# Splitting two tile drains and reordering one: tiles 3 and 7 in halves, V pair 4 ahead of a gelu

## Chip, cores, metric

One core of a Trainium2 chip. The metric is the device time of the whole program in microseconds (us), median of several executions. "Span" is the time from the first to the last instruction in a profile; it is some 1.7 us shorter than the metric.

## The reference

`x` is 2048 tokens by 448 features, bf16. It is normalised, and the result goes through a linear attention (A) and a shifted MLP (B):

```python
xn = layernorm(x)
# A: 16 heads of 28
q, k, v = split(xn @ wqkv)
phi(t)  = concat(softmax(t @ w_phi), softmax(-t @ w_phi))
o       = (phi(q) @ (phi(k).T @ v)) / (phi(q) @ phi(k).sum() + 1e-6)
# B
h  = gelu(layernorm(xn) @ w1)           # quarters of h shifted by 1, -1, 2, -2 tokens
x1 = xn + shift(h) @ w2
out = x + o @ wo + x1 + gelu(layernorm(x1) @ w3) @ w4
```

The change lies in the opening stretch, about 7 to 17 us: xn is transposed tile by tile, and `xn @ wv` ("V pairs" of two 128-token tiles) and `xn @ w1` ("WA", "WC", "WD": blocks of w1's columns, for groups of four tiles) run as the tiles arrive.

## The kernel before

The kernel records all instructions for five engines in program order and derives the semaphores from the buffers that they touch. Nothing is timed: each engine works through its own list, and what one line of the list costs depends on what it waits for.

Transposes of one tile go through TensorE into a pair of PSUM banks (eight small ones, in two row halves), and ScalarE copies them to `xnT`:

```python
def xn_t(i, b, j=0):                       # b: bank pair
    t = pairs[b][:, :].bitcast(BF16).rearrange("p (h x) -> p h x", h=2)
    for kc in range(KC):                   # KC = 4
        at = 256 * j + 64 * kc
        for h, (lo, hi) in enumerate((LO, HI)):
            R.tr(t[:, h, at:at + 64], xn[lo:hi, i, 128 * kc:128 * kc + 128], ident[lo:hi, lo:hi])

def xn_e(i, b, n=1, eng="ACT", cuts=(0, KC)):
    ...
                for c0, c1 in zip(cuts, cuts[1:]):
                    R.act(to[:, c0:c1], fr[:, c0:c1], ACT.Copy)
```

A V pair accumulates two tiles in the two banks of its pair. Matmuls of the lower and the upper 64 rows run side by side, in different banks; then they swap banks ("late"):

```python
def early():
    row_pairs(side(0, LO, (0, 1)), side(1, HI, (0, 1)), True)
    if i > 3:
        mid()
def mid():
    row_pairs(side(0, LO, (2, 3)), side(1, HI, (2, 3)))
return early, lambda: row_pairs(side(1, LO, (0, 1, 3)), side(0, HI, (0, 2, 3))), mid
```

`V(i, 0)`, `V(i, 2)`, `V(i, 1)` are early, middle and late. `v_out` is ScalarE's drain of a V pair, `wa_out` and `wc_out` are gelus that drain w1's blocks. The bank pairs: tile 7's transposes and V pair 6 both use pair 3; V pair 4 and tiles 8, 9 use pair 2; WA of groups 0 and 1 use pair 0.

The dependency tracker keeps PSUM by bank: a write to a bank waits for every reader and writer of that bank on another engine, and a matmul on one row half waits for the other half's last write to the same bank.

```python
vps = {i: v_pair(i, b) for i, b in ((0, 2), (2, 3), (4, 2), (6, 3), (8, 2), (10, 2), (14, 3))}
play([(spin, 3, 256), (xn_T, 2, 0), V(0, 0), (xn_T, 3, 1), V(0, 2), V(0, 1),
      V(2, 0), V(2, 2), (v_out, 0, 2), (xn_T, 4, 1), WA(0, 0),
      V(2, 1), (v_out, 2, 3), (xn_T, 5, 2), WA(0, 1), WC(0, 0), (xn_T, 6, 3), WC(0, 1), (wc_out, 0, 1),
      V(4, 0), (xn_T, 7, 3), (wa_out, 0, 0), V(4, 1), (v_out, 4, 2), V(6, 0),
      WC(1, 0), V(6, 1), (v_out, 6, 3), (xn_T, 8, 2, 2), WA(1, 0), ...])
```

The softmax here doesn't subtract the row's maximum and nothing guards it: scores larger than these inputs give would overflow.

## Time and profile before

| | before |
|---|---|
| device time, median of 3 | 173.45 us (173.34 to 173.59) |
| span in the profile | 171.7 us |
| TensorE busy | 167.9 us, 98% |
| ScalarE busy | 83.7 us, 49% |

TensorE bounds the kernel. How to read such a profile here: a matmul's record is longer than what it occupies of the array, so gaps of TensorE are counted from start to start. A bracket at the end of a row of the timeline gives the idle time of that engine before the row and what ended it. Weight loads ("PEld") run ahead of matmuls, so their idle time is an upper bound of what the array lost.

The prediction below shows TensorE's rows. ScalarE's, from the timeline of the kernel before (start, length, engine, line, operation, output from input, shapes), are what parts two and three of the change rearrange:

```profile
14.38 0.60 ACT L208 ACTIVATE xnT<-bank 128x512 bf16<-128x512 bf16 x1 [0.16 <-PE bank L204]
14.87 1.02 ACT L208 ACTIVATE hT<-bank 128x1024 bf16<-128x1024 f32 x1
15.78 0.92 ACT L208 ACTIVATE vaug<-bank 128x896 bf16<-128x896 f32 x1
17.01 0.92 ACT L208 ACTIVATE vaug<-bank 128x896 bf16<-128x896 f32 x1 [0.31 <-PE bank L200]
```

The rows are tile 7's copy, the gelu of w1 group 0, the drain of V pair 4 and that of V pair 6. The gelu stands between tile 7's copy and V pair 4's drain.

### The profile page before, as it was taken

The page shows a single profiled execution, that of the slowest core. Times are in us where ns is not written, and L with a number is a line of the kernel's source. Part 1 is how long each engine was busy: PE and PEld are TensorE (multiplying, and loading weights), DVE is VectorE, ACT ScalarE, POOL GpSimd, SP SyncE. Part 2 cuts the span into 40 slices and gives each one's busy share as a digit, 9 for nine tenths or more (in the row PEclk, how much of TensorE's full clock was granted, in tenths as well). Part 3 has the DMA queues.
Part 4 walks back from the last instruction along what each step waited for, and adds up shares of the span by engine and source line. Part 5 has one row for each costly group of instructions (what it writes and reads, how often), then busy time and mean ns, then how long its engine had stood idle before and what let it go on. Part 6 is the DMA issues. An engine that isn't in the chain of part 4 may idle for free.

```text
span 171.7 us, 5220 instructions
## 1 busy us (share of the span) xinstructions
PE 167.9 (98%) x2269; PEld 89.9 (52%) x2269; DVE 112.6 (66%) x259; ACT 83.7 (49%) x102; POOL 91.6 (53%) x130
## 2 busy tenths in 40 slices
PE   7999999999999999999999999999999999999994
PEld 5455576444555554554545555545545555545553
DVE  4799986368999999837678953446417425474621
ACT  4868863988777887847225222224203222224000
POOL 3676560024799999750749388540721714523740
PEclk9999999999999999999999999999999999999999
DMA  4996541239943011122103732035311220314331
GB/s 131 320 270 86 135 102 42 55 45 376 379 144 64 4 31 34 31 46 50 34 2 75 79 63 60 30 86 107 80 36 50 61 57 4 84 31 34 84 88 53
DMA packets 32679, 15.21 MB, mean 89 GB/s; under 512 B 23952, under 2 KB 32016, under 8 KB 32656
## 3 DMA queue, kind: packets, MB, share of 16 engines
q1 hardware_dynamic: 32224, 14.62, 34.9%
q8 instruction: 18, 0.29, 0.8%
q10 hardware_dynamic: 432, 0.26, 0.5%
q14 instruction: 5, 0.04, 0.1%
HBM read 7.14 MB, written 1.84 MB: 52 GB/s over the span
## 4 chain that ended last, share of the span: by engine, by line
PE 94%; DVE 2%; issue 1%; POOL 1%
PE bank L200 93%; PE bank L204 1%; POOL rs L212 1%; DVE vaug L212 1%; DVE st L212 0%; DVE xn L212 0%; POOL mv L212 0%; DVE mv L212 0%; DVE gT L212 0%
## 5 line engine op out<-in xcount | busy, mean ns | idle before, releaser
L208 ACT ACTIVATE phik<-bank 128x1024 bf16<-128x1024 f32 (+1 forms) x44 | 42.3, 984 | 60.3 <-PE bank L200 60.2
L200 PE MATMUL bank<-gT,w 64*128 64x512 bf16 x392 | 50.0, 377 | 0.0
L212 DVE TENSOR_TENSOR vaug<-bank,vaug 128x464 f32<-128x464 f32 (+3 forms) x65 | 32.7, 512 | 22.5 <-PE bank L200 20.9
L200 PE MATMUL bank<-w,phik 64*128 64x448 bf16 (+3 forms) x434 | 45.2, 343 | 0.0
L212 POOL TENSOR_TENSOR xnT<-vaug 128x196 bf16<-128x196 f32 (+1 forms) x32 | 18.1, 587 | 45.4 <-DVE vaug L212 45.4
L200 PEld LDWEIGHTS bank<-w,phik 64*128 64x128 bf16 (+1 forms) x434 | 22.4, 94 | 20.8 <-issue 0.4
L645 POOL TENSOR_TENSOR phik<-phik,rks 128x1792 bf16<-128x1792 bf16 (+1 forms) x9 | 25.8, 2877 | 11.1 <-DVE rks L212 10.3
L200 PEld LDWEIGHTS bank<-gT,w 64*128 64x128 bf16 x392 | 17.6, 94 | 17.5 <-ACT phik L208 0.4
L212 POOL TENSOR_TENSOR vaug<-xn,xtok 128x448 f32<-128x448 bf16 x16 | 16.2, 1034 | 0.2 <-DVE vaug L212 0.2
L212 DVE TENSOR_REDUCE ksum<-phik 128x64 f32<-128x1792 bf16 x8 | 16.1, 2011 | 0.0
L212 DVE RECIPROCAL vaug<-bank 128x16 f32<-128x16 f32 x16 | 4.1, 257 | 17.8 <-PE bank L200 17.8
L212 POOL TENSOR_TENSOR rs<-mv,mhalf 128x1 f32<-128x1 f32 (+2 forms) x20 | 13.1, 658 | 3.3 <-DVE mv L212 1.8
L200 PE MATMUL bank<-xnT,wpq 64*128 64x512 bf16 x112 | 14.7, 376 | 0.0
L200 PE MATMUL bank<-wo,xnT 64*128 64x448 bf16 (+3 forms) x110 | 13.6, 343 | 0.0
L200 PE MATMUL bank<-wv,xnT 64*128 64x448 bf16 x112 | 13.2, 350 | 0.1
L200 PE MATMUL bank<-w,hT 64*128 64x448 bf16 x112 | 13.2, 349 | 0.0
L200 PE MATMUL bank<-wpk,xnT 64*128 64x448 bf16 x112 | 13.2, 349 | 0.0
L200 PE MATMUL bank<-xnT,w 64*128 64x512 bf16 (+2 forms) x168 | 12.6, 306 | 0.0
L212 DVE TENSOR_TENSOR xn<-bank,xn 128x512 bf16<-128x512 f32 (+1 forms) x16 | 9.2, 619 | 3.0 <-PE bank L200 3.0
L208 ACT ACTIVATE hT<-bank 128x512 bf16<-128x512 f32 (+1 forms) x10 | 7.4, 770 | 4.0 <-PE bank L200 4.0
L212 DVE BATCH_NORM_STATS2 st<-xn 128x6 f32<-128x448 bf16 x16 | 9.3, 580 | 0.0
L212 POOL TENSOR_SCALAR g_tok<-xn,rs 128x512 bf16<-128x512 bf16 x12 | 9.1, 772 | 0.3
(68 smaller groups left out, 166.7 us busy)
## 6 DMA issues: line engine op xcount, KB each, us to landing
w<-in_B_w_dram SPq DMA_DIRECT2D x2, 896.0 KB, 5.8
out_dram<-vaug SPq DMA_DIRECT2D x15, 112.0 KB, 1.9
w<-in_B_w_dram SPq DMA_DIRECT2D x1, 1568.0 KB, 11.2
xtok<-in_A_x_dram SPq DMA_DIRECT2D x2, 448.0 KB, 6.0
wv<-in_A_wqkv_dram SPq DMA_DIRECT2D x2, 224.0 KB, 4.4
xtok<-in_A_x_dram SPq DMA_DIRECT2D x2, 224.0 KB, 4.7
w<-in_B_w_dram SPq DMA_DIRECT2D x2, 224.0 KB, 4.8
wo<-in_A_wo_dram SPq DMA_DIRECT2D x2, 224.0 KB, 6.7
```

The costliest lines, as they stand in the source:

```text
L200: self.op("PE", lambda e: e.matmul(out, lhsT, rhs, start=start, stop=stop, skip_group_check=True), [out], [lhsT, rhs], tile=self._tile(lhsT))
L204: self.op("PE", lambda e: e.transpose(out, in_, ident), [out], [in_, ident], tile=self._tile(in_))
L208: self.op("ACT", lambda e: e.activation(out, in_, func, **kw), [out], [in_] + aps)
L212: self.op(eng, lambda e: getattr(e, name)(out, *args, **kw), [out], aps)
L645: R.op(pool, lambda e, h=h: e.tensor_tensor(ph[:, h, :], ph[:, h, :], rb[:, h, :], op=ALU.mult), [ph[:, h, :]], [ph[:, h, :], rk, *(g_tok[ ...
```

## The change

The intent: give TensorE tile 3's first half sooner and use the second half to fill a wait; let V pair 6 start on tile 7's first half; free V pair 4's banks before the gelu, since tile 8 needs them.

```diff
-        def xn_t(i, b, j=0):
+        def xn_t(i, b, j=0, cut=(0, KC)):
...
-            for kc in range(KC):
+            for kc in range(*cut):
...
+        def xn_Th(i, b, *cut):
+            xn_t(i, b, 0, cut)
+            xn_e(i, b, cuts=cut)
...
-        play([(spin, 3, 256), (xn_T, 2, 0), V(0, 0), (xn_T, 3, 1), V(0, 2), V(0, 1),
+        play([(spin, 3, 256), (xn_T, 2, 0), V(0, 0), (xn_Th, 3, 1, 0, 2), V(0, 2), (xn_Th, 3, 0, 2, KC), V(0, 1),
...
-              V(4, 0), (xn_T, 7, 3), (wa_out, 0, 0), V(4, 1), (v_out, 4, 2), V(6, 0),
+              V(4, 0), (lambda: xn_T(7, 3, cuts=(0, 2, KC)),), V(4, 1), (v_out, 4, 2),
+              (wa_out, 0, 0), V(6, 0),
```

## The prediction

> **What bounds the kernel now.** I read the engine table of the page first, then the chain of work that ended last, then the waits inside the stretch that the change touches, then the timeline of that stretch engine by engine. The engine table and the clock row of the page:
>
> ```profile
> PE 167.9 (98%) x2269; PEld 89.9 (52%) x2269; DVE 112.6 (66%) x259; ACT 83.7 (49%) x102; POOL 91.6 (53%) x130
> PEclk9999999999999999999999999999999999999999
> ```
>
> TensorE is busy for 98% of the span. The clock row must be read beside it: no slice is throttled, so nothing is to be had from the clock. The chain in order of time (start, length, what):
>
> ```profile
> 6.87 0.42 DVE xn L212
> 7.29 0.05 issue
> 7.33 0.29 PE bank L204 x8
> ...
> 19.32 4.28 PE bank L200 x60
> 23.60 0.23 PE bank L204 x16
> 23.84 145.65 PE bank L200 x1943
> ```
>
> From 7.33 us on the chain stays on TensorE to 169.49 us. All edits lie between about 7.8 and 17 us. The change adds and removes no matmul and no transpose, so all that it can win is idle time of TensorE inside that stretch, and only if a later wait doesn't take it back. The waits between 7 and 24 us (total, times, longest):
>
> ```profile
> PEld bank L204 <- DVE xn L212: 1.0, 3, 0.4
> PEld bank L200 <- PE bank L200: 0.5, 1, 0.5
> PEld bank L200 <- ACT xnT L208: 0.4, 1, 0.4
> PEld bank L204 <- issue: 0.3, 1, 0.3
> PEld bank L204 <- DVE wpk L212: 0.2, 1, 0.2
> ```
>
> These are waits of the weight loads, which run ahead of the matmuls; the array loses less. I count the loss from matmul starts: a pair of 448-column matmuls on the two row halves occupies 0.19 us (V pair 4's second step starts pairs at 14.29, 14.48 and 14.67), though each is recorded as 0.35 long. The places, from the timeline:
>
> ```profile
> 7.85 0.17 PEld L204 LDWEIGHTS bank<-ident,xn 64*128 64x128 bf16 x8 [0.29 <-DVE xn L212]
> 8.58 1.06 PEld L200 LDWEIGHTS bank<-wv,xnT 64*128 64x128 bf16 x14 [0.50 <-PE bank L200]
> 9.51 0.41 DVE L212 TENSOR_SCALAR xn<-xtok,mv,rs 128x512 bf16<-128x512 bf16 x1 [0.23 <-POOL rs L212]
> 9.97 0.17 PEld L204 LDWEIGHTS bank<-ident,xn 64*128 64x128 bf16 x8 [0.33 <-DVE xn L212]
> 15.03 0.11 PEld L200 LDWEIGHTS bank<-wv,xnT 64*128 64x128 bf16 x4 [0.44 <-ACT xnT L208]
> 16.81 0.32 PEld L204 LDWEIGHTS bank<-ident,xn 64*128 64x128 bf16 x16 [0.29 <-issue]
> 23.41 0.31 PEld L204 LDWEIGHTS bank<-ident,xn 64*128 64x128 bf16 x16 [0.24 <-DVE wpk L212]
> ```
>
> Real array gaps: 0.22 us before 8.58 (last pair of V pair 0's middle step starts at 8.17, so the array is free at 8.36); 0.05 before 9.97 (9.73 + 0.19); 0.17 before 15.03 (14.67 + 0.19); 0.04 before tile 8's first transpose at 16.84 (16.61 + 0.19); 0.06 before 23.41 (23.16 + 0.19). Together 0.54 us, 0.3% of 173.45. That bounds the gain before anything else is asked: 2% would be 3.5 us.
>
> **What the Trainium skill says.** "ScalarE: Activation LUTs", section "What ACT_TABLE_LOAD costs": an ACTIVATE with immediate scale costs 186 ns plus 0.833 ns per element, and neighbours overlap by about 93 ns. The trace agrees: 512 columns took 0.60 us (formula 0.61), 256 columns 0.38 (formula 0.40), and tile 1's two halves started 0.28 apart (6.81 and 7.09). "PSUM — Partial Sum Buffer", section "PSUM bank collisions raise a hardware error": software must guard PSUM by bank, since a different address of the same bank still collides, and different row tiles must not write one bank at once. This kernel's dependency tracker does that: a write waits for every reader of the bank, and a matmul on the other row half waits for its predecessor's end; the trace shows the latter as 0.50 us before 8.58. "TensorE: Matmul & The Clock Gate", section "Wait — 56ns, not 53.3ns?": warm matmuls start N/2.4 GHz + 2.5 ns apart, 189 ns for 448 columns; the trace has 0.19.
>
> **The change, part by part.**
>
> *Tile 3 in halves.* Before: V pair 0 early, eight transposes, middle step, late step. After: four transposes ahead of the middle step, four behind it. The eight took 0.10 us of issue (weight loads 7.85, next step's loads 7.95), so four fewer make the middle step start about 0.05 to 0.06 earlier: 7.92 instead of 7.98. The first four still wait for VectorE's tile 3 (7.39 + 0.41 = 7.80), so no more than that. The late step waits for the end of the middle step's matmuls on the opposite row halves: 8.58 becomes 8.52. The second four write the other bank pair, which ScalarE's copy of tile 2 reads until 7.67 + 0.60 = 8.27; they go at about 8.33, inside that wait. ScalarE does tile 3 in two copies, about 8.19 to 8.57 and 8.61 to 8.99; V pair 2 needs them at 9.11 and 9.48. No new wait, 0.06 gained at 8.52. But the next transposes, tile 4's, wait for VectorE at 9.51 + 0.41 = 9.92, seen at 9.97. VectorE's tile 4 hangs on POOL's power and on VectorE's own statistics, none of which waits for TensorE here. So tile 4 stays at 9.97; the gap before it grows from 0.05 to 0.11. Worth on the path: 0.00.
>
> *Tile 7 in halves.* ScalarE's copy runs 14.38 to 14.98 and releases V pair 6's first step at 15.03. After: 14.38 to 14.76 and 14.66 to 15.04. The intent must be to start V pair 6 on the first half. But V pair 6 accumulates in bank pair 3, and tile 7's transposes lie in bank pair 3: its first matmul overwrites what the second copy still reads. So it waits for both, and starts at 15.04 + 0.05 = 15.09. Cost: 0.06.
>
> *V pair 4 drained first.* Before, ScalarE does the gelu (14.87 to 15.89), then V pair 4 (15.78 to 16.70). Tile 8's transposes need V pair 4's banks, so they can't start before about 16.76, and are seen at 16.81/16.84 where the array was free at 16.80: 0.04 lost. After: V pair 4's matmuls end at 14.67 + 0.35 = 15.02, its drain runs 15.08 to 16.00, and that gate is gone. Gain: 0.04. The gelu moves to about 15.89 to 16.91. It holds bank pair 0, which w1 group 1 wants: seen at 17.07 before, free after at about 16.97. Not a new bound as long as TensorE isn't more than 0.1 early.
>
> *Sum.* At tile 8's first transpose: V pair 6 at 15.09 instead of 15.03, no gate: 16.80 + 0.06 = 16.86 against 16.84, so +0.02. From there to tile 10 the array is full, so tile 10's transposes move by the same +0.02, and VectorE's copy of tiles 10 and 11 (seen at 19.36), which starts the chain of statistics, POOL power, tiles 12 to 15 and weight copy that releases TensorE at 23.41, moves with it. Total 0.00 + 0.06 - 0.04 = +0.02 us on 173.45, below the 0.25 us spread of the three runs.
>
> **The rivals.** First, the intent works: V pair 6 starts when the array is free, at 14.86, so 0.17 early. Then w1 group 1 would want bank pair 0 at about 16.86 and get it from the late gelu at 16.97, which leaves 0.10; VectorE's copy of tiles 10 and 11 can't start before its statistics end at 19.30 (0.06 before 19.36), and the wait at 23.41 passes on 0.06. Time about 173.39. The shared bank pair speaks against it. Second, tile 3's 0.06 reaches the end: that needs VectorE's tile 4 to come earlier, which nothing in the change does; also about 173.39. Third, the later gelu becomes the bound: if ScalarE's three drains take 0.2 more than added up here, w1 group 1 starts at about 17.2 and the time is about 173.6; against it, the gelu's 1.02 us and the drain's 0.92 us are steady. Fourth, an unseen effect on the order of transfers: the weight loads near 19 us and the stores are issued by another queue at times that this change does not touch.
>
> **Range and chances.** Predicted 173.45 us: the +0.02 of the sum, set against a small chance of the first two rivals (about -0.06) and of something favourable that the sum misses. The range 173.20 to 173.68 is the spread seen before (173.34 to 173.59) widened by about 0.1 each way for the rivals and another set of runs. Within 2%: 0.985. Faster by 2% would need six times the idle time counted here: 0.01. Slower: 0.005, for a wait missed altogether.
>
> **What would show it right or wrong.** In the changed profile: V pair 0's late step about 0.06 earlier, near 8.52, yet tile 4's transposes still near 9.97, with a longer wait for VectorE; V pair 6's weight loads still waiting for ScalarE's xnT, to about 15.09, after the second half's copy; if they start near 14.86, the bank argument is wrong. Tile 8's loads without the wait to 16.81; the gelu near 15.9; w1 group 1's matmuls within 0.05 of 17.07, and if they wait for ScalarE's hT, the third rival holds. The wait at 23.41 still there. A change of more than 0.3 us in either direction would mean that a part of the program beyond 24 us reacts, which nothing here predicts.

## The result

| | before | changed |
|---|---|---|
| device time, median of 6 | 173.46 us (173.34 to 173.59) | 173.49 us (173.38 to 173.63) |
| span in the profile | 171.7 us | 171.7 us |
| TensorE busy | 167.9 us | 167.6 us |

The ratio is 1.0001, 95% interval 0.9988 to 1.0014: no difference. A ratio here is the mean time of one kernel's fast runs over that of the other's in the same rounds, so not quite the ratio of the two medians. Executions over 1.5% slower than the fastest of the same kernel are left out of the means.

The page counts the same 2269 matmuls as before and 104 instructions of ScalarE in place of 102: the two extra copies. The timeline of the changed kernel, TensorE's weight loads that answer to those in the prediction:

```profile
7.82 0.12 PEld L204 LDWEIGHTS bank<-ident,xn 64*128 64x128 bf16 x4 [0.29 <-DVE xn L212]
8.28 0.11 PEld L204 LDWEIGHTS bank<-ident,xn 64*128 64x128 bf16 x4 [0.29 <-ACT xnT L208]
8.49 1.06 PEld L200 LDWEIGHTS bank<-wv,xnT 64*128 64x128 bf16 x14
9.93 0.17 PEld L204 LDWEIGHTS bank<-ident,xn 64*128 64x128 bf16 x8 [0.38 <-DVE xn L212]
15.05 0.49 PEld L200 LDWEIGHTS bank<-wv,xnT 64*128 64x128 bf16 x8 [0.51 <-ACT xnT L208]
16.64 0.46 PEld L204 LDWEIGHTS bank<-ident,xn 64*128 64x128 bf16 x16
23.38 0.31 PEld L204 LDWEIGHTS bank<-ident,xn 64*128 64x128 bf16 x16 [0.25 <-DVE wpk L212]
```

V pair 0's late step (8.49) is earlier than before (8.58), yet tile 4 (9.93) waits for VectorE as it did, only longer: 0.38 in place of 0.33. V pair 6 (15.05) waits for ScalarE longer than before, 0.51 in place of 0.44. Tile 8's loads (16.64) have no wait left. Tile 14 (23.38) waits for VectorE's weight copy as before.

ScalarE, the four rows that answer to those above, in their new order:

```profile
14.34 0.66 ACT L208 ACTIVATE xnT<-bank 128x256 bf16<-128x256 bf16 x2 [0.16 <-PE bank L204]
15.03 0.92 ACT L208 ACTIVATE vaug<-bank 128x896 bf16<-128x896 f32 x1
15.84 1.02 ACT L208 ACTIVATE hT<-bank 128x1024 bf16<-128x1024 f32 x1
17.03 0.92 ACT L208 ACTIVATE vaug<-bank 128x896 bf16<-128x896 f32 x1 [0.17 <-PE bank L200]
```

Two copies of 256 columns took 0.66 us where one of 512 took 0.60, and V pair 6 started at 15.05, when the second of them had ended at 15.00. The chain of waits of the changed kernel now steps off TensorE at that place, which it did not before:

```profile
14.18 0.14 PE bank L204 x8
14.32 0.02 issue
14.34 0.67 ACT xnT L208 x2
15.01 0.05 issue
15.05 1.94 PE bank L200 x22
```

**A common origin for all runs.** The first loads land a little earlier or later in each execution: tile 2's first transpose, ahead of every edit, stands at 7.33 us before and 7.30 after, and over the runs below between 7.16 and 7.83. It moves everything behind it, and so the device time. Positions below are counted from it. "End" is the start of the last VectorE addition.

| | V pair 0 late | tile 4 | V pair 6 | tile 8 | tile 10 | tile 14 | end |
|---|---|---|---|---|---|---|---|
| before | 1.25 | 2.64 | 7.70 | 9.51 | 11.58 | 16.08 | 162.18 |
| changed | 1.20 | 2.64 | 7.75 | 9.53 | 11.60 | 16.09 | 162.21 |
| tile 3 alone | 1.19 | 2.63 | 7.69 | 9.50 | 11.57 | 16.07 | 162.17 |
| tile 7 alone | 1.25 | 2.64 | 7.76 | 9.57 | 11.64 | 16.15 | 162.25 |
| drain alone | 1.25 | 2.64 | 7.69 | 9.47 | 11.54 | 16.03 | 162.14 |
| changed, tile 7 whole | 1.19 | 2.63 | 7.69 | 9.46 | 11.53 | 16.02 | 162.13 |

### The profile page after: what moved, and what is told of

The parts are those of the page before. It is cut to its first block, busy times and chain, and to the rows that moved or that the text cites. A ratio compares the mean times of both kernels' runs of the same rounds, so it can differ in the third digit from the quotient of the medians.

```text
span 171.7 us, 5222 instructions
## 1 busy us (share of the span) xinstructions
PE 167.6 (98%) x2269; PEld 89.7 (52%) x2269; DVE 112.5 (66%) x259; ACT 83.9 (49%) x104; POOL 91.5 (53%) x130
## 3 DMA queue, kind: packets, MB, share of 16 engines
HBM read 7.14 MB, written 1.84 MB: 52 GB/s over the span
## 4 chain that ended last, share of the span: by engine, by line
PE 94%; DVE 2%; issue 1%; POOL 1%; ACT 0%
PE bank L200 93%; PE bank L204 1%; POOL rs L212 1%; DVE vaug L212 1%; ACT xnT L208 0%; DVE st L212 0%; DVE xn L212 0%; POOL mv L212 0%; DVE mv L212 0%; DVE gT L212 0%
## 5 line engine op out<-in xcount | busy, mean ns | idle before, releaser
L212 DVE TENSOR_TENSOR vaug<-bank,vaug 128x464 f32<-128x464 f32 (+3 forms) x65 | 32.7, 512 | 22.5 <-PE bank L200 20.9
L212 POOL TENSOR_TENSOR xnT<-vaug 128x196 bf16<-128x196 f32 (+1 forms) x32 | 18.0, 585 | 45.6 <-DVE vaug L212 45.6
L212 POOL TENSOR_TENSOR vaug<-xn,xtok 128x448 f32<-128x448 bf16 x16 | 16.2, 1031 | 0.2 <-DVE vaug L212 0.2
L212 DVE TENSOR_REDUCE ksum<-phik 128x64 f32<-128x1792 bf16 x8 | 16.1, 2011 | 0.0
L212 DVE RECIPROCAL vaug<-bank 128x16 f32<-128x16 f32 x16 | 4.1, 257 | 17.8 <-PE bank L200 17.8
L212 POOL TENSOR_TENSOR rs<-mv,mhalf 128x1 f32<-128x1 f32 (+2 forms) x20 | 13.1, 657 | 3.3 <-DVE mv L212 1.8
L212 DVE TENSOR_TENSOR xn<-bank,xn 128x512 bf16<-128x512 f32 (+1 forms) x16 | 9.2, 618 | 3.0 <-PE bank L200 3.0
L212 DVE BATCH_NORM_STATS2 st<-xn 128x6 f32<-128x448 bf16 x16 | 9.3, 580 | 0.0
L212 POOL TENSOR_SCALAR g_tok<-xn,rs 128x512 bf16<-128x512 bf16 x12 | 9.1, 764 | 0.3
```

The source lines that it names most:

```text
L212: self.op(eng, lambda e: getattr(e, name)(out, *args, **kw), [out], aps)
```

## The experiments

Two things on the times first. In the sessions of these runs, some executions of most kernels, the one before included (2 of 7, 3 of 11 and 3 of 11 executions in three sessions), took about 175 to 177 us and not 173.5; most of them still count as fast by the 1.5% rule and widen the intervals to half a per cent and more. What they probably are is discussed after run 8. At 2%, runs 1 to 8 are all "same" as the kernel before; only the intervals of runs 5, 6 and 8 (ratios 1.0099, 1.0084 and 1.0100) lie above 1. So, by a cut of my own, I read times from executions under 174.5 us where a run has enough of them, and verdicts mainly from positions in profiles, which were repeatable to about 0.02 us.

### 1. Tile 3 in halves alone

```diff
 # against the changed kernel
-  V(4, 0), (lambda: xn_T(7, 3, cuts=(0, 2, KC)),), V(4, 1), (v_out, 4, 2), (wa_out, 0, 0), V(6, 0),
+  V(4, 0), (xn_T, 7, 3), (wa_out, 0, 0), V(4, 1), (v_out, 4, 2), V(6, 0),
```

> Tile 3 in halves alone, the rest as before. All positions are counted from tile 2's first transpose (7.33 us in the profile of before, 7.30 in that of the changed kernel), which lies ahead of every edit. My theory: V pair 0's late step 0.05 to 0.06 earlier (1.19 to 1.20 instead of 1.25), tile 4's first transpose unmoved at 2.64 because VectorE and POOL set it, and everything later as before (V pair 6 at 7.70, tile 8 at 9.51, tile 14 at 16.08); time ratio 1.000. Rival (the gain reaches the end): tile 4 and all later positions 0.05 earlier.

Measured: 173.40 us median of 4 (before, its five executions under 174.5: 173.47). Late step at 1.19, tile 4 at 2.63, end at 162.17 against 162.18. The 0.06 us is won and lost again within 1.5 us, in the wait for VectorE's tile 4. The rival, a gain that reaches the end, falls.

### 2. Tile 7 in halves alone

```diff
 # against the kernel before
-  V(4, 0), (xn_T, 7, 3), (wa_out, 0, 0), ...
+  V(4, 0), (lambda: xn_T(7, 3, cuts=(0, 2, KC)),), (wa_out, 0, 0), ...
```

> Tile 7's copy in two halves alone, the rest as before. My theory (V pair 6 overwrites the bank pair that both halves read): V pair 6 starts about 0.06 later, at 7.76 instead of 7.70, only after the second copy has ended; the gelu is 0.06 later too and so is V pair 4's drain, so tile 8's first transpose is at about 9.57 instead of 9.51; the 0.06 is passed on to tile 10 and partly lost in the slack ahead of tile 14. Time ratio 1.000 to 1.001. Rival (the first half releases V pair 6): V pair 6 at about 7.53 and tile 8 not earlier than before, since V pair 4's drain comes no sooner.

Measured: 173.55 us median of 4. V pair 6 at 7.76, tile 8 at 9.57, as expected; tile 14 at 16.15 and the end at 162.25, so the cost of 0.07 us arrives whole. I had expected part of it to be lost ahead of tile 14; nothing was. The wait of V pair 6's weight loads for ScalarE is the one of the changed kernel, 0.51.

### 3. V pair 4's drain ahead of the gelu alone

```diff
 # against the kernel before
-  V(4, 0), (xn_T, 7, 3), (wa_out, 0, 0), V(4, 1), (v_out, 4, 2), V(6, 0),
+  V(4, 0), (xn_T, 7, 3), V(4, 1), (v_out, 4, 2), (wa_out, 0, 0), V(6, 0),
```

> V pair 4's drain ahead of the gelu alone. My theory: V pair 6 unmoved at 7.70; tile 8's weight loads no longer wait, its first matmul at 9.47 instead of 9.51; w1 group 1 and tile 10 about 0.04 earlier; VectorE's copy of tiles 10 and 11 at most 0.06 earlier and tile 14 at most 0.04 earlier. Time ratio 1.000. Rival (the later gelu is the new bound): w1 group 1 starts with a wait for ScalarE's hT and later than 9.74.

Measured: executions at 173.45, 173.86 and 173.89, and one at 175.36. The profiled one had tile 2's first transpose at 7.83, half a microsecond later than before, which is in its 173.89; counted from there, tile 8 is at 9.47 and the end at 162.14, 0.04 earlier than before. w1 group 1 had no wait for the gelu. So this part is worth 0.04 us, by positions; the times can't show it.

### 4. The changed kernel with tile 7 copied whole

```diff
 # against the changed kernel
-  (lambda: xn_T(7, 3, cuts=(0, 2, KC)),)
+  (xn_T, 7, 3)
```

> The changed kernel with tile 7 copied whole. My theory (the split costs 0.06 and buys nothing): V pair 6 back at 7.70 instead of 7.75, tile 8 at 9.47 instead of 9.53, tile 14 within 0.04 of 16.08. Time ratio to before 1.000. Rival (the split helps something else): tile 8 or tile 14 later than in the changed kernel.

Measured: 173.19 and 173.87, and two executions at 174.88 and 175.26. V pair 6 back at 7.69, tile 8 at 9.46, end at 162.13: 0.08 earlier than the changed kernel. With runs 1 to 3 the parts add up: -0.01, +0.07 and -0.04 make +0.02, and the changed kernel stands at +0.03.

### 5. V pair 6 in a bank pair of its own

```diff
 # against the changed kernel: bank pairs 1 and 3 change places from V pair 6 to tile 14
-  V: ... (6, 3) ...   WC: (1, 1)   fold: ((1, 0, 1), (1, 2, 3), (0, 0, 3), (0, 2, 1))
+  V: ... (6, 1) ...   WC: (1, 3)   fold: ((1, 0, 3), (1, 2, 1), (0, 0, 3), (0, 2, 1))
-  (v_out, 6, 3) ... (wc_out, 1, 1) ... (xn_T, 10, 3, 2, "DVE") ... (xn_T, 14, 1, 2)
+  (v_out, 6, 1) ... (wc_out, 1, 3) ... (xn_T, 10, 1, 2, "DVE") ... (xn_T, 14, 3, 2)
-  WC(2, 0), FO(0, 0, 0), WC(2, 1), (wc_out, 2, 0), FO(0, 2, 0), FO(0, 0, 1), FO(0, 2, 1)
+  WC(2, 0), FO(0, 2, 0), WC(2, 1), (wc_out, 2, 0), FO(0, 0, 0), FO(0, 2, 1), FO(0, 0, 1)
```

> The changed kernel with V pair 6 moved to bank pair 1, so that it no longer shares a bank pair with tile 7's transposes; w1's third block of group 1 and the later users of bank pairs 1 and 3 up to tile 14 change places with it. My theory (the shared bank pair is what keeps V pair 6 waiting for both halves): V pair 6 starts about 0.2 us earlier, at 7.53 to 7.57 counted from tile 2's first transpose, with no wait for ScalarE worth naming. Then most of the 0.2 is given back: w1 group 1 waits for the gelu's bank pair (about 9.66 to 9.70), VectorE's statistics hold back its copy of tiles 10 and 11, and tile 14 is at most 0.06 earlier than 16.08. Time ratio 0.999 to 1.001. Rival (V pair 6 waits for something else, such as V pair 4's end): it stays at 7.75.

Measured: the weight loads of V pair 4's late step and V pair 6's first step are now one uninterrupted row of 14:

```profile
14.22 1.06 PEld L200 LDWEIGHTS bank<-wv,xnT 64*128 64x128 bf16 x14
```

V pair 6 starts at 14.79, at 7.54, as expected: 0.21 earlier than in the changed kernel, with no wait. The halves of tile 7 do what they were meant to do as soon as the bank pair isn't shared. Tile 8 is at 9.31; then the loads of w1 group 1 come at 16.89, 0.33 after tile 8 where the 16 transposes need 0.23: 0.10 given back to the gelu's bank pair, as expected. Tile 10 is at 11.49 and tile 14 at 15.98, 0.11 earlier than in the changed kernel; I had allowed 0.06 against 16.08 and got 0.10, a miss with the same cause as that of run 7.

And yet the time was 174.71 to 176.94 us in all four executions. The profile shows a wait that none of the earlier ones had. TensorE's timeline, and the clock row of the page:

```profile
28.27 4.95 PE L200 MATMUL bank<-xnT,w 64*64 64x256 bf16 x63 [1.84 <-DMA xnT<-xn]
```
```profile
PEclk9999997999999999999999999999999999999999
```

w1's last block waits 1.84 us for the transposes of tiles 12 and 13, which are done by transfer and not by TensorE; and then the clock falls. This is taken up after run 8.

### 6. The gelu later still

```diff
 # against the changed kernel
-  (wa_out, 0, 0), V(6, 0), WC(1, 0), V(6, 1), (v_out, 6, 3),
+  V(6, 0), WC(1, 0), V(6, 1), (v_out, 6, 3), (wa_out, 0, 0),
```

> The changed kernel with the gelu of w1 group 0 put off once more, behind V pair 6's drain: the suspected cost of the third part, made large. My theory: the gelu runs at about 17.84 to 18.86 and holds bank pair 0 until then, so w1 group 1 starts with a wait for ScalarE's hT at about 18.9 us instead of 17.06, 1.85 later, and since nothing later has so much slack the kernel loses 1.5 to 1.9 us: ratio 1.009 to 1.011. Rival (bank pair 0 is not what matters there): w1 group 1 unmoved, ratio 1.000.

Measured: 175.36 us median of 4 (175.10 to 175.36). w1 group 1:

```profile
18.87 1.52 PEld L200 LDWEIGHTS bank<-xnT,w 64*128 64x128 bf16 x20 [1.81 <-ACT hT L208]
```

It starts at 18.87 with a wait of 1.81 us for the gelu, tile 10 is at 13.46 (1.86 later than in the changed kernel) and the end at 164.05 (1.84 later). There is no wait for a transfer in this profile and the clock is full, so these 175.36 are the gelu's doing. Bank pair 0 is the limit of the third part: the change puts off the gelu by as much as fits (it ends at 16.86, w1 group 1 starts at 17.03 in the changed kernel), and beyond that every microsecond counts in full.

### 7. Tile 4's transposes behind the first step of w1 group 0

```diff
 # against the changed kernel
-  (v_out, 0, 2), (xn_T, 4, 1), WA(0, 0),
+  (v_out, 0, 2), WA(0, 0), (xn_T, 4, 1),
```

> The changed kernel with tile 4's transposes moved behind w1 group 0's first step, so that TensorE has work while VectorE finishes tile 4. My theory (the 0.06 of tile 3's halves is lost in the wait for VectorE's tile 4): that wait is gone and w1 group 0's first step starts at about 2.55 instead of 2.77 counted from tile 2's first transpose (0.11 of idle and 0.10 of transposes moved); V pair 6, tile 8 and w1 group 1 come 0.11 earlier, the last held to about 0.10 by the gelu or not at all; but VectorE's copy of tiles 10 and 11 comes at most 0.05 earlier and tile 14 stays within 0.05 of 16.08. Ratio 0.9995 to 1.000. Rival (nothing between tile 10 and tile 14 takes it back): tile 14 0.11 earlier, ratio 0.9994.

Measured: four executions between 173.21 and 173.31 (median 173.27; before, eight under 174.5, median 173.41), two at 174.95 and 176.75. The wait for VectorE's tile 4 is gone; V pair 6 is at 7.62, tile 8 at 9.40, tile 10 at 11.47 and tile 14 at 15.96: 0.13 earlier than in the changed kernel at all of the last four. I had expected tile 14 to stay within 0.05 of 16.08, because VectorE's copy of tiles 10 and 11 could not come much earlier. It came 0.13 earlier, at 19.17. So the rival was right on tile 14, and the step that failed is told below. The profiled execution was the slow one of 176.75, so its end says nothing; the four fast ones agree with a gain of about 0.13, but at this spread of times they don't prove it.

### 8. Both waits for VectorE removed

```diff
 # against the changed kernel, tile 7 whole, tile 4 later as in run 7
+                if t and not m:
+                    R.act(wpk[:, m:m + 2, :], two(2 * b)[:, :, 0:D], ACT.Copy)
+                    return
                 if t:
                     R.ew(dve, "tensor_copy", wpk[:, m:m + 2, :], two(2 * b)[:, :, 0:D])
```

> As the run with tile 4's transposes later, with tile 7 copied whole, and with the first of the two weight copies that release tile 14 taken from VectorE to ScalarE, which idles there. My theory (the wait for VectorE at 23.41 is the second place that takes gains back): the wait for VectorE's wpk is gone, tile 14 starts 0.2 to 0.25 earlier than 16.08 (0.11 at tile 4, 0.04 at tile 8, 0.06 ahead of tile 14), and the end of the span comes earlier by about as much if nothing after 24 us takes it: ratio 0.9985 to 0.999, which five rounds may just show. Rival (a third place later takes it back): tile 14 earlier by 0.2, the end unmoved, ratio 1.000.

Measured: tile 14 at 15.84, 0.24 earlier than before, with no wait left. But 174.38 to 176.91 us in six executions. In the profiled one TensorE waits for the transfer again:

```profile
28.25 4.96 PE L200 MATMUL bank<-xnT,w 64*64 64x256 bf16 x61 [1.81 <-DMA xnT<-xn]
```

### What took 1.8 us and more in runs 5, 7 and 8

The three profiles with this wait are those of runs 5, 7 and 8; the profiles of the two kernels and of runs 1 to 4 and 6 end without it. Run 8 by stretches of a microsecond shows what follows it (stretch, its length, busy time and instructions of PE, PEld, DVE, ACT and POOL, then the granted clock, the transfers' share and GB/s):

```profile
28.00:29.00 1.00, 0.75 (x20) 0.78 (x24) 0.28 (x5) 0.00 (x0) 0.00 (x0) 0.71 0.10 27
29.00:30.00 1.00, 1.00 (x25) 1.00 (x19) 0.00 (x0) 0.14 (x1) 0.00 (x0) 0.50 0.15 33
30.00:31.00 1.00, 1.00 (x14) 0.28 (x7) 0.00 (x0) 0.96 (x2) 0.00 (x0) 0.50 0.40 94
```

TensorE stands from 26.44 to 28.25, and its clock is halved for some three microseconds after that: the loss doubles, to 3.5 us of span. The halving does not follow from the length of the gap alone. In run 6 TensorE stood for 1.70 us (17.17 to 18.87) and the clock stayed at 1.00, while in run 7 it stood for 1.67 us and the clock fell to 0.50. And in the record of the single executions of runs 1 to 8 and of the kernel before, those of 174.5 to 175.7 us list a mean clock of 1.0, and those of 176.5 to 177 us list 0.99, as the three profiled ones do. What decides it is not shown.

Where are the transfers? The two transposes of xn are issued by SyncE, after eight weight transposes and after w2. SyncE's timeline of the kernel before, and of run 8:

```profile
18.91 2.76 SPq L218 DMA_DIRECT2D w<-in_B_w_dram  x3
21.72 2.77 SPq L215 DMA_TRANSPOSE xnT<-xn  x2
```
```profile
19.36 2.63 SPq L218 DMA_DIRECT2D w<-in_B_w_dram  x3
22.03 2.82 SPq L215 DMA_TRANSPOSE xnT<-xn  x2
```

Counted from tile 2's first transpose, the issue starts at 14.39 before, at 14.70 in run 8, 14.79 in run 5 and 14.90 in run 7; in the profiles of runs 1 to 4 and of the changed kernel it starts at 13.86 to 14.41, with no wait. (In run 6 TensorE itself is 1.86 later.) From issue to landing they took a median of 2.5 to 3.0 us in the seven profiles without the wait (3.0 before, 2.6 in the changed kernel) and 3.7 to 4.0 in the three with it (3.7 in run 7, 4.0 in runs 5 and 8). Two things set the issue: SyncE must be through with w2, and VectorE must have written xn of tile 12. In runs 5, 7 and 8 w2 came last (in run 8 xn was written by about 21.0, w2's issue ended at 21.99); in run 6 and in runs 9 to 12 it was VectorE (SyncE waited 3.1 to 3.7 us for xn).

How much of the wait is TensorE's earliness? Little. In run 8 TensorE wanted the second transpose by 26.44; at the same place in the list the kernel before was at 26.62, and its second transpose, issued at 23.03, took 3.3 us to land, to about 26.3. In run 8 it was issued at 23.35 and took 4.8, to about 28.2 (estimates from the issue rows and the times to landing). So 0.2 us comes from the faster TensorE and about 1.8 from the later landing, of which 1.5 is a longer time in flight. In the stretch from 22 to 24 us the transfers' share of the 16 engines was 0.75 to 1.05 in the three profiles, and 0.28 to 0.69 in those of the two kernels and runs 1 to 4: the densest microsecond of the traffic in this stretch lay before 22 us there (223 GB/s from 21 to 22 in the kernel before) and behind it here (281 GB/s from 22 to 23 in run 8). Why it came later is not shown. Nor is it shown that the edits made it late: over 174.5 us were 9 of 10 executions of runs 5 and 8, but only 2 of 6 of run 7 and 8 of 29 of the kernel before.

### 9 to 12. Loading w2 later

The last four runs move w2's load (first used at 36.1 us) out of the way of these transposes, in the kernel before, in runs 8 and 5, and in a combination of runs 5, 7 and 8.

```diff
-        R.dma(w2[:, 0:3, :], B_w2[0:384, :]...)       # ahead of the transposes of xn
-        for p0 in (0, 64):
-            R.dma(w2[p0:p0 + 64, 3, :], B_w2[384:448, :])
...
         halo()
+        R.dma(w2[:, 0:3, :], B_w2[0:384, :]...)
+        for p0 in (0, 64):
+            R.dma(w2[p0:p0 + 64, 3, :], B_w2[384:448, :])
         load_rest()
```

The kernel before with w2 later:

> The kernel before, with the load of w2 (first used at 36.1 us) issued after the exchange of hT's shifted columns instead of ahead of the transposes by transfer of tiles 12 and 13. Theory from the runs so far: the executions near 175.3 and 176.9 us, of the kernel before as of the others, are those in which these two transposes land after w1's last block wants them (seen in three profiles as 1.7 to 1.8 us of wait for the transfer, with the clock falling to 0.5 after it in those that were profiled); they queue behind w2. With w2 later they are issued about 0.5 us earlier and land sooner: no execution over 174.5 us in 6, median 173.4 to 173.5. Rival (those executions come from something else): 1 to 3 of 6 still near 175.

Run 8 with w2 later:

> The run that removed both waits for VectorE, with w2 loaded later. Theory: its 1.8 us of wait for the transfer and its clock of 0.5 go away, and its gain of 0.24 us at tile 14 reaches the end: 173.2 us, all executions within 0.3 of each other, ratio to the fast runs of before 0.9985. Rival (the wait for the transfer comes from these edits, not from w2's place in the queue): still 174.5 or more.

Run 5 with w2 later:

> The run with V pair 6 in its own bank pair, with w2 loaded later. Theory: V pair 6 and tile 14 where they were in that run (about 0.2 and 0.1 us earlier than in the changed kernel) and now the end 0.1 earlier too: 173.35 us. Rival: still over 174.5.

The combination:

> The changed kernel with V pair 6 in its own bank pair, tile 4's transposes later, the first weight copy on ScalarE and w2 loaded later: the version that the runs point to. Theory: the gains at tile 14 add up to 0.3 us (0.11 at tile 10 from the bank pair after the gelu's wait, 0.13 from tile 4, 0.1 from the weight copy, less what the gelu's bank pair takes back) and reach the end: 173.1 to 173.2 us, ratio 0.998. Rival (they don't add up, since the gelu holds bank pair 0): as the run with both waits removed, 173.2 to 173.25.

Measured: 179.75, 179.79, 181.37 and 180.69 us (medians of 6, 6, 4 and 6). All four are over 3% slower, and every expectation of a time failed, through a mistake of mine that the profile shows at once. SyncE's and TensorE's timelines of the kernel before with w2 later:

```profile
36.60 2.94 SPq L218 DMA_DIRECT2D w<-in_B_w_dram  x5
```
```profile
39.96 1.81 PE L200 MATMUL bank<-w,hT 64*128 64x448 bf16 x8 [3.58 <-DMA w<-in_B_w_dram]
```

I had put the load behind the exchange of hT's shifted columns, taking SyncE to be there at about 30 us. But that exchange itself waits for w1's last gelus and ended at 36.56 in this profile, so w2 was issued only at 36.60, when it was already wanted, and TensorE waited 3.58 us (3.9 to 4.1 in the others), with the clock at 0.50 afterwards (from 40 to 46 us here).

What these runs still show, up to 30 us: in all four profiles the transposes of xn are issued at 21.0 to 21.3, at 13.67 to 13.85 counted from tile 2, land in 2.6 to 2.7 us, and no wait for them appears. In run 8's version with w2 later, TensorE reaches the attention phase at 22.39, where the kernel before is at 22.56: 0.17 of the 0.24 won at tile 14 is kept there. In the combination tile 14 is at 15.78, 0.30 earlier than before, as expected, but its attention phase starts at 22.80, 0.24 later: moving the fold (w_phi multiplied into the weights of k and q, wpk and wpq) into other banks, which is part of run 5's edit, brought waits of weight loads for VectorE's wpq of 0.9 us in all. Run 11, with the same edit, has them too, and run 9, without it, has not. So run 5's edit has a price behind tile 14, which its own profile hides under the wait for the transfers. So no version was found that beats the two kernels by its time, and that the executions near 175 us vanish without w2 ahead of the transposes stays open, since no run gives it free of the new wait. That their loss comes from this wait is shown for profiled executions of runs 5, 7 and 8; for the unprofiled ones of the kernel before it is an inference from the same size.

## Why the prediction was right

It said 173.45 us for a measured 173.49, and worked out +0.02 us for a +0.03 in the trace. The time alone proves little: executions of one kernel scatter by 0.25 us, so any sum of small terms near zero would have met it, and 0.01 us in the trace is within what repeats. What speaks for the mechanism is that each part's own term was measured, in runs 1 to 4. By its steps:

- **No more than 0.54 us to win.** Consistent with all runs: the largest gain at tile 14 was 0.30 (the combination), and by its time no kernel was shown to be faster. The count left one gap out: the answer on waits has a sixth line for weight loads, `PEld bank L204 <- DVE st L212: 0.2, 1, 0.2`, ahead of tile 6 (12.77). The last pair before it starts at 12.63 and pairs of 256 columns start 0.11 apart, so the array is free at 12.74, and tile 6 begins at 12.80: 0.06 more, about 0.60 in all. The drain of V pair 2, from the same bank pair, ends at 12.66; no run tried to move it.
- **Tile 3: 0.06 won at the late step, 0.00 at the end.** Late step 0.05 earlier (0.06 in run 1), tile 4 unmoved at 2.64, end unmoved in run 1. The second four transposes fitted inside the wait, as said. Run 7 confirms the reason: with tile 4 out of the way, positions from V pair 6 on move by 0.13 (more than 0.06, since the whole gap ahead of tile 4 goes).
- **Tile 7: +0.06.** V pair 6 moved by +0.05 in the changed kernel and +0.06 in run 2. The reason, the shared bank pair, is shown by run 5.
- **V pair 4's drain: -0.04.** Run 3 has -0.04 at tile 8 and at the end.
- **The gelu doesn't bind.** It ends at 16.86 and w1 group 1's loads come at 17.03; run 6 shows what would have been the price.
- **VectorE's copy of tiles 10 and 11 comes at most 0.06 earlier.** This side estimate, in the first rival, was too small. I took the statistics' recorded end, 19.30, as the earliest start; but VectorE started the copy 0.10 after the start of that 0.18 us statistic. Run 8's timeline:

```profile
19.10 0.18 DVE L212 BATCH_NORM_AGGREGATE mv<-st 128x2 f32<-128x6 f32 x1
19.20 0.75 DVE L212 COPY xnT<-bank 128x512 bf16<-128x512 bf16 x2
```

  That is 11.87 from tile 2, where the kernel before copies at 12.03: the slack was at least 0.16. The copy starts 0.45 after tile 10's first transpose in both (18.91 to 19.36 before, 18.75 to 19.20 in run 8), so TensorE still set it. It is why run 7 moved tile 14 by 0.13. The sum of the prediction doesn't contain it, as it had no gain to pass on.
- **Tile 14 takes gains back.** Said as a limit; in runs 2, 3, 4 and 7 shifts of -0.13 to +0.07 passed through whole, because the chain that releases tile 14 starts from TensorE's own tile 10 and moves with it. It delays, but it didn't absorb.
- **Nothing beyond 24 us reacts.** True of the changed kernel. Not true in general: in the profiles of runs 5, 7 and 8 the transposes by transfer landed after TensorE wanted them, at about 26 us. The prediction's fourth rival, transfers issued "at times that this change does not touch", was named and set aside; the experiments met it, though most of that wait is not due to an earlier TensorE.

## What to carry to other kernels

Splitting a drain helps a consumer only if it doesn't write the banks that the second half still reads: look up the bank of the producer and that of the consumer before the instruction counts. For each gain ask which engine sets the next start; a gain ahead of a start that another engine sets is gone, unless that engine's chain begins at yours. And look how long before their use the transfers land, before shaving tenths: here the margin in the kernel before was 0.3 us at most (an estimate: landed at about 26.3, wanted by 26.62), and missing it brought a wait of 1.8 us in run 8, which with the slower clock behind it cost 3.5.

## What the Trainium skill lacked or had wrong

- "TensorE: Matmul & The Clock Gate", section "HAM oscillation — how this bites in real kernels": its rule is to leave no idle gap over about 3.4 us. Here that is not safe: in run 8 a gap of 1.8 us between matmuls (26.44 to 28.25) was followed by a granted clock of 0.71 in the microsecond from 28 and 0.50 in the two after it. Nor does such a gap always do it: after 1.70 us in run 6 the clock was 1.00.
- "ScalarE: Activation LUTs", section "What ACT_TABLE_LOAD costs": its formula gives 0.71 us for two overlapping copies of 256 columns and 0.61 for one of 512 (estimates from 186 ns, 0.833 ns per element and 93 ns of overlap); measured 0.66 and 0.60. So a split would cost 0.09 by the formula and cost 0.06. The prediction took 0.06 from the trace.
- "PSUM — Partial Sum Buffer", section "PSUM bank collisions raise a hardware error": this kernel keeps its rule to guard by bank; the page does not say what follows for split drains, that a second half of 0.38 us keeps the next accumulation out of the bank (V pair 6 at 7.75, and at 7.54 with banks of its own).
